# Attention in a fixed order of slots on every engine, four transposed-probability buffers, the query scale in the exponential, and the first three gates on GpSimd

## The chip, the cores and the metric

One core of one Trainium2 chip. Time is device microseconds (us) of the one core, the median of the runs shown; lower is better. The engines of the core are TensorE (PE in the rows; its weight loads PEld), VectorE (DVE), ScalarE (ACT), GpSimd (POOL) and SyncE (SP, which only issues DMAs here).

## What is computed

Three layers in one launch: attention with a mask from hashed buckets, a mixture of eight experts with two experts for each token, and a feed-forward layer with a rational activation. The change lies in the first layer and in the choice of experts.

```python
# attention: q, k, v are [2, 8, 768, 64]; proj is [64, 6]
q_bucket = sum(((q @ proj) > 0) * 2**arange(6)); k_bucket likewise
scores = where(q_bucket[:, :, :, None] == k_bucket[:, :, None, :], 0.125 * q @ k.T, -1e9)
attn = exp(scores - max(scores)); attn = attn / (sum(attn) + 1e-9)
x = (attn @ v).transpose(0, 2, 1, 3).reshape(1536, 512)
# choice of experts, 8 of them
noisy = x @ w_gate + log1p(exp(x @ w_noise)) * noise
top2, weights = the two largest of noisy, and their softmax
x = sum over a token's two experts e: weight * relu(x @ w1[e]) @ w2[e]     # 512 -> 1024 -> 512
# last layer
h = x @ w_in; out = (P(h) / Q(|h|)) @ w_out                                # 512 -> 2048 -> 512
```

## The kernel before

**Precision.** Products are taken in float32r (one pass over PE) with each operand as a high part, rounded, and a low part, the rest; a product is two or three such passes. So nearly every tile is made twice: ACT copies the high part, DVE or GpSimd subtracts it from the original.

**Units and slots.** Attention is cut into 32 units, a head's 384 queries of one batch (a "group" of tokens, four of them), and each unit into three query tiles of 128. One tile is the work of one slot, 96 in all. A tile goes through five stages, each a slot or more after the one before: `score` (4 products of 384 columns, the bucket bits as extra rows of the operands, so that a key of another bucket gets a far lower score), the row maximum and from it scale and bias (`sb`) on DVE, `expo` (the exponential on ACT), then for two of the unit's six key tiles `ptrans` (3 transposes each into one PSUM tile, a copy of the high part on ACT, the low part on DVE, both into a tile `PT`), and `av` (4 products with the values). The PSUM tiles: two for scores (`ps_s`), three small ones (`ps_1`) that transposes, bucket bits and `fold` share, one for the output (`ps_o`).

**Beside the slots.** For each head the keys are split (`k_split`: ACT and GpSimd) and their bits made (`k_bits`, 4 products, one DVE instruction and two DMAs); for each unit the queries are split (`q_split`: GpSimd multiplies by 0.125, ACT copies the high part with the same scale, GpSimd subtracts), and for two units the bits (`q_bits2`, 4 products, one ACT instruction and two DMAs). After a unit's last `av` its output is copied (`oT`), the sums are inverted (`rec`, two DVE instructions), `fold` (3 products) adds high and low parts and makes the gates' columns, and DVE scales them into the rows of the experts (`xg` or `io`). After a group's last head its `Gate` chooses the experts: some 25 small instructions of DVE, 4 of ACT, 7 products, and 6 indirect DMAs of GpSimd that scatter the rows.

**What sets the order.** `run` calls the stages slot by slot; but in attention the order on each engine is set by the compiler's scheduler, which lists instructions by priority and its own times and so may shift one between the instructions of another stage. The order is fixed in the program; at run time each engine goes through its list and waits at the first instruction whose inputs are not there. From the second expert layer's start on the order of PE, ACT and DVE is the program's (`manual_schedule`).

## Time and profile before

| | us |
|---|---|
| median of three runs | 927.43 (927.17 to 929.77) |
| span of the profiled execution, first to last instruction | 918.6 |
| median less span: start and end, outside the span | 8.8 |
| from the first exponential's start to the last one's, 95 slots | 12.5 to 268.6: 256.1 |
| from there to the first product with the first expert's last rows | 268.6 to 284 |
| experts and last layer | 284 to 918.6: 634.6 |

The profiled execution has no time of its own beside its span, so what lies around the span is taken as the median less the span. In the profile, "busy" is the time in which at least one instruction of the engine runs; instructions of one engine can overlap by a little, so that the distance of two starts is shorter than a duration. The mean duration of a group of instructions includes whatever holds one back after it has started.

### The profile page before, as it was taken

Reading aid. Unit: us, or ns where it says so; the run is one execution under the profiler, and the core shown is the slowest. Engines: PE = TensorE matmul, PEld = TensorE weight load, DVE = VectorE, ACT = ScalarE, POOL = GpSimd, SP = SyncE. Lnnn points to the kernel's source line nnn. Section 1 sums busy time; section 2 is a strip of 40 time slices with the busy share of each in tenths; the row PEclk is TensorE's granted clock in tenths of the full one; section 3 lists DMA queues with packets and bytes.
Section 4 is the critical chain, followed back from the end, with each engine's and each line's share of the span. In section 5 each row is a group of like instructions: output and inputs, shape, how many; then the busy total and the mean of one; then the engine's idle time right before and its main releaser. Section 6 shows DMA issues by size and latency. Waiting matters only on the chain. (4 is left out here: it accounts for less than half of the span.)

```text
span 918.6 us, 14182 instructions
## 1 busy us (share of the span) xinstructions
PE 876.3 (95%) x4725; PEld 777.0 (85%) x4725; DVE 772.3 (84%) x1484; ACT 656.2 (71%) x1302; POOL 353.1 (38%) x328
## 2 busy tenths in 40 slices
PE   6999999998999999999999999997989999999997
PEld 4888999898987888888888888876777899989995
DVE  8999999999985777777777776635999999999996
ACT  6888888898973555555545555525988988988885
POOL 6667444644504243433344332032363242222221
PEclk9999999999999999999999999998999999999999
DMA  8888852431313877879687776534221010000000
GB/s 247 229 236 230 265 132 56 151 92 56 131 42 130 252 246 249 252 244 293 224 261 242 231 249 223 177 106 136 71 81 35 36 46 1 36 1 1 35 1 34
DMA packets 89948, 132.22 MB, mean 144 GB/s; under 512 B 9296, under 2 KB 56400, under 8 KB 89872
## 3 DMA queue, kind: packets, MB, share of 16 engines
q1 hardware_dynamic: 86032, 118.70, 41.8%
q0 software_dynamic: 3840, 12.59, 4.3%
q8 instruction: 38, 0.62, 0.3%
q14 instruction: 38, 0.31, 0.1%
HBM read 88.20 MB, written 33.55 MB: 133 GB/s over the span
## 5 line engine op out<-in xcount | busy, mean ns | idle before, releaser
L757 PE MATMUL ps<-xsT,big 128*128 128x448 f32 x768 | 168.2, 368 | 0.0
L776 PE MATMUL s<-big,hT 128*128 128x512 f32 x633 | 154.5, 391 | 0.7 <-DVE hT L762 0.7
L757 PEld LDWEIGHTS ps<-xsT,big 128*128 128x128 f32 x768 | 142.2, 188 | 12.0
L1006 PE MATMUL ps<-x2T,big 128*128 128x384 f32 x768 | 147.5, 340 | 2.8 <-DVEq L891 1.5
L1058 PE MATMUL s<-big,gT 128*128 128x512 f32 x528 | 141.0, 398 | 8.6 <-ACT gT L1041 4.4
L1006 PEld LDWEIGHTS ps<-x2T,big 128*128 128x128 f32 x768 | 137.0, 190 | 8.3 <-ACTq L891 1.9
L1042 POOL TENSOR_TENSOR gT<-uu,gT 128x384 fp32r<-128x384 f32 x64 | 71.7, 1120 | 187.3 <-ACT gT L1041 169.0
L776 PEld LDWEIGHTS s<-big,hT 128*128 128x128 f32 x633 | 118.8, 188 | 23.3 <-DVE hT L762 1.1
L643 DVE TENSOR_TENSOR big<-wraw,big 128x1024 fp32r<-128x1024 f32 x76 | 98.9, 1306 | 36.3 <-ACT big L639 36.3
L1058 PEld LDWEIGHTS s<-big,gT 128*128 128x128 f32 x528 | 96.3, 188 | 33.9 <-ACT gT L1041 9.2
L761 ACT ACTIVATE hT<-ps 128x384 fp32r<-128x384 f32 x114 | 40.7, 357 | 102.3 <-DVE hT L762 82.2
L687 POOL TENSOR_SCALAR convok<-convok 128x512 f32<-128x512 f32 x32 | 49.5, 1546 | 154.8 <-ACT convok L681 150.3
L288 PE MATMUL o<-PT,vhl 128*128 128x384 f32 x384 | 105.3, 368 | 3.2 <-DVE PT L278 2.8
L278 DVE TENSOR_TENSOR PT<-ps,PT 128x384 fp32r<-128x384 f32 x192 | 103.9, 549 | 5.3 <-ACT PT L277 4.2
L267 ACT ACTIVATE probs<-s,sb 128x768 f32<-128x768 f32 x96 | 95.5, 995 | 16.3 <-DVE sb L259 15.3
L277 ACT ACTIVATE PT<-ps 128x384 fp32r<-128x384 f32 x192 | 93.0, 492 | 16.6 <-PE o L288 8.5
L275 PE MATMUL ps<-ident,probs 128*128 128x128 f32 x576 | 95.5, 275 | 5.7 <-DVE PT L278 3.4
L251 PE MATMUL s<-big,qT 128*128 128x384 f32 x384 | 95.2, 362 | 2.9 <-ACT probs L267 1.6
L258 DVE TENSOR_REDUCE mx<-s 128x1 f32<-128x768 f32 x96 | 91.0, 948 | 7.0 <-PE s L251 6.5
L275 PEld LDWEIGHTS ps<-ident,probs 128*128 128x128 f32 x576 | 72.0, 140 | 17.9 <-DVE PT L278 5.2
L639 ACT ACTIVATE big<-wraw 128x1024 fp32r<-128x1024 f32 x80 | 83.9, 1056 | 2.3 <-DMA wraw<-in_moe_w_dram 2.3
L1023 DVE SCALAR_TENSOR_TENSOR uu<-uu,na,hh 128x384 f32<-128x384 f32 x64 | 73.5, 1149 | 1.9
(188 smaller groups left out, 1495.6 us busy)
## 6 DMA issues: line engine op xcount, KB each, us to landing
wraw<-in_moe_w_dram SPq DMA_DIRECT2D x64, 512.0 KB, 5.0
wraw<-in_moe_w_in_dram SPq DMA_DIRECT2D x16, 512.0 KB, 4.9
wraw<-in_moe_w_out_dram SPq DMA_DIRECT2D x16, 512.0 KB, 3.8
xs<-zero SPq DMA_DIRECT2D x14, 512.0 KB, 4.5
io<-xs SPq DMA_DIRECT2D x14, 448.0 KB, 4.6
qraw<-in_q_dram SPq DMA_DIRECT2D x32, 192.0 KB, 2.7
y<-io SPq DMA_DIRECT2D x24, 256.0 KB, 3.4
kraw<-in_k_dram SPq DMA_DIRECT2D x15, 384.0 KB, 3.7
```

The source lines that it names most:

```text
L251: nc.tensor.matmul(ps[:, c, 0:384], T[:, r, q], R[:, r, c * 384:(c + 1) * 384], start=(r == 1), stop=(r == 0))
L258: nc.vector.tensor_reduce(m[:, 1:2], ps[:, :, 0:384], axis=AX.XY, op=ALU.max, negate=True)
L267: nc.scalar.activation(pt.rearrange("p (c k) -> p c k", c=2), ps[:, :, 0:384], AF.Exp, bias=sb[:, 1:2], scale=sb[:, 0:1], accum_out=st["su ...
L275: nc.tensor.transpose(ps[:, i * P:(i + 1) * P], self.S[u]["P"][i][:, kt * P:(kt + 1) * P], E.ident)
L277: nc.scalar.activation(t[:, 0, :], ps[:, 0:384], AF.Copy)
L278: nc.vector.tensor_tensor(t[:, 1, :], ps[:, 0:384], t[:, 0, :].bitcast(F32), op=ALU.subtract)
L288: nc.tensor.matmul(self.O[u][:, 0:384], self.K[b, h]["vhl"][:, kt, :], t[:, r, :], start=(kt == 0 and r == 0), stop=(kt == 5 and r == 1))
L643: (lo or nc.vector).tensor_tensor(t[:, 1, :], raw, t[:, 0, :].bitcast(F32), op=ALU.subtract)
L757: nc.tensor.matmul(ps[:, 0:CAP], w[:, a, c, fs], x[:, c, b, :], start=(n == 0), stop=(n == 11))
L776: nc.tensor.matmul(self.acc[e][j], h[a][:, j * P:(j + 1) * P] if j < 3 else tail, w[:, b, :], start=(f == 0 and a + b == 0), stop=(f == 7 ...
L1006: nc.tensor.matmul(ps, w[:, a, c, fs], x[:, b, c, :], start=(n == 0), stop=(n == 11))
L1058: nc.tensor.matmul(ps, g[:, a, j * P:(j + 1) * P], w[:, b, f % 2, :], start=(f == 0 and a + b == 0), stop=(f == 15 and a == 1))
```

## The change

Five things, all up to the end of attention:

1. **Order.** Attention runs inside `manual_schedule` for PE, ACT, DVE and GpSimd: each slot's instructions stand on each engine in the order in which the loop calls them. Functions that mixed engines are cut so that each part can have its place: `ptrans` into `ptrans`, `high` (ACT) and `low` (DVE), `score` into `score` and `most` (DVE), `q_bits2` and `k_bits` into products and `_out`, `av`'s end into `out` and `recip`, `fold` into `fold` and `rows`, the gates' steps into finer ones. The slots of keys, queries and gates get new rules (`ks`, `vs`, `kb`).
2. **The maximum.** It goes to an unused column of the score's own PSUM tile, and scale and bias come from two instructions in place of one. The constant tiles `mx` go away.
3. **The query scale.** The 0.125 moves into that scale, so `q_split` loses GpSimd's multiplication; `BIG` grows to match.
4. **Buffers.** `PT` has four in place of three; the tile `spacer` moves to a pool that outlives attention.
5. **Gates.** For the first three groups the small elementwise steps run on GpSimd (`self.eng`), some as two instructions where DVE has a fused one; their scatters are one per slot. The split of the last group's rows for the first expert goes head by head.

```diff
+LAG = 1
+PTB = 4
-BIG = float(2 ** 28)
+BIG = float(2 ** 31)
...
     def q_split(self, u, eng=None):
...
-            q = self.ap.tile([P, 384], F32, name="qs", bufs=2)
-            nc.gpsimd.tensor_scalar(q, raw, 0.125, None, op0=ALU.mult)
-            nc.scalar.activation(T[:, 0, :], raw, AF.Copy, scale=0.125)
-            nc.gpsimd.tensor_tensor(T[:, 1, :], q, T[:, 0, :].bitcast(F32), op=ALU.subtract)
+        nc.scalar.activation(T[:, 0, :], raw, AF.Copy)
+        (eng or nc.gpsimd).tensor_tensor(T[:, 1, :], raw, T[:, 0, :].bitcast(F32), op=ALU.subtract)
...
-        m = E.mx[self.nm % len(E.mx)]
-        self.nm += 1
+        self.S[u][i] = ps
+
+    def most(self, u, i):
+        nc, E = self.nc, self.E
+        ps = self.S[u][i]
+        m = ps[:, 0, 384:385]
         sb = self.ap.tile([P, 2], F32, name="sb", bufs=6)
-        nc.vector.tensor_reduce(m[:, 1:2], ps[:, :, 0:384], axis=AX.XY, op=ALU.max, negate=True)
-        nc.vector.scalar_tensor_tensor(sb, m[:, 1:2].to_broadcast([P, 2]), BIG, m,
-                                       op0=ALU.is_le, op1=ALU.mult)
+        nc.vector.tensor_reduce(m, ps[:, :, 0:384], axis=AX.XY, op=ALU.max, negate=True)
+        nc.vector.tensor_scalar(sb[:, 0:1], m, BIG, 0.125, op0=ALU.is_le, op1=ALU.mult)
+        nc.vector.tensor_tensor(sb[:, 1:2], m, sb[:, 0:1], op=ALU.mult)
...
-        t = self.ap.tile([P, 2, 384], F32R, name="PT", bufs=3)
+        self.PT[u, kt] = ps
+
+    def high(self, u, kt):
+        nc, ps = self.nc, self.PT[u, kt]
+        t = self.ap.tile([P, 2, 384], F32R, name="PT", bufs=PTB)
         nc.scalar.activation(t[:, 0, :], ps[:, 0:384], AF.Copy)
+        self.PT[u, kt] = (ps, t)
+
+    def low(self, u, kt):
+        nc, (ps, t) = self.nc, self.PT[u, kt]
         nc.vector.tensor_tensor(t[:, 1, :], ps[:, 0:384], t[:, 0, :].bitcast(F32), op=ALU.subtract)
...
-        for s in range(max(max(pe), max(free), 3 * N + 8) + 1):
-            pend.extend(pe.get(s, []))
-            for f, a in free.get(s, []):
-                f(*a)
-            stage(self.ptrans, s - 4, 2)
-            stage(self.score, s, 1)
-            stage(self.ptrans, s - 4, 2, 1)
-            stage(self.expo, s - 1, 1)
-            stage(self.av, s - 5, 2)
-            misc()
-            stage(self.av, s - 5, 2, 1)
-            misc()
-            while len(pend) > 7:
-                misc()
...
+        with self.tc.manual_schedule(engines=MANUAL | {mybir.EngineType.Pool}):
+            for s in range(max(max(d) for d in (bits, dve, act, outs, free)) + 1):
+                run(free, s)
+                run(outs, s)
+                stage(self.ptrans, s - 4, 2)
+                stage(self.high, s - 4, 2)
+                stage(self.ptrans, s - 4, 2, 1)
+                stage(self.high, s - 4, 2, 1)
+                stage(self.expo, s - 1, 1)
+                run(act, s)
+                stage(self.score, s, 1)
+                run(dve, s)
+                stage(self.low, s - 4, 2)
+                stage(self.low, s - 4, 2, 1)
+                stage(self.most, s, 1)
+                run(bits, s)
+                stage(self.av, s - 4 - LAG, 2)
+                stage(self.av, s - 4 - LAG, 2, 1)
...
+        self.eng = tc.nc.gpsimd if n < 3 else tc.nc.vector
...
         if self.n < 3:
-            return [self.choose, self.noisy, self.top, self.rank, self.rank2, self.scatter]
+            return [(free, 4, self.choose), (act, 4, self.soft), (free, 5, self.noisy), (dve, 6, self.top),
+                    (bits, 7, self.rank), (dve, 7, self.count), (dve, 8, self.rank2), (free, 9, self.weigh),
+                    (act, 10, self.weigh2), (dve, 11, self.weigh3)] + [(free, 10 + i, self.scatter, i) for i in range(6)]
```

The lists `free`, `outs`, `act`, `dve` and `bits` hold what a slot does beside the stages; a gate's pieces stand as (list, slots after its unit's end, function). Three places show what that does to the order. The first is DVE in the middle of a batch of heads. Before, the maximum (L258), `sb` (L259) and the low parts (L278) of different tiles stand between one another:

```order
L278 TENSOR_TENSOR PT<-ps_982,PT 128x384 [waits Activation_49]
L258 TENSOR_REDUCE mx_126<-s 128x1 [waits PE_49]
L278 TENSOR_TENSOR PT<-ps_998,PT 128x384 [waits Activation_49]
L259 SCALAR_TENSOR_TENSOR sb<-mx_126 128x2 [waits DVE_49]
L314 TENSOR_TENSOR lgh<-ps_1009,rec 128x3x16 [waits PE_49]
L319 TENSOR_TENSOR io<-ps_1009,rec 128x2x64
L319 TENSOR_TENSOR io<-ps_1009,rec 128x64
L278 TENSOR_TENSOR PT<-ps_1022,PT 128x384 [waits Activation_49]
L258 TENSOR_REDUCE mx_127<-s 128x1 [waits PE_49]
L278 TENSOR_TENSOR PT<-ps_1037,PT 128x384 [waits Activation_49]
L259 SCALAR_TENSOR_TENSOR sb<-mx_127 128x2 [waits DVE_49]
```

Of the change, at about the same place (L295 is the low part, L266 the maximum, L268 and L269 scale and bias, L201 the keys' bits):

```order
L295 TENSOR_TENSOR PT<-ps_1062,PT 128x384 [waits Activation_49]
L266 TENSOR_REDUCE s<-s 128x1 [waits PE_49]
L268 TENSOR_SCALAR sb<-s 128x1 [waits DVE_49]
L269 TENSOR_TENSOR sb<-s,sb 128x1 [waits DVE_49]
L201 TENSOR_SCALAR big_903<-ps_1084,kthr,kmul 128x384 [waits PE_49]
L295 TENSOR_TENSOR PT<-ps_1096,PT 128x384 [waits Activation_49]
L295 TENSOR_TENSOR PT<-ps_1102,PT 128x384 [waits Activation_49]
L266 TENSOR_REDUCE s<-s 128x1 [waits PE_49]
L268 TENSOR_SCALAR sb<-s 128x1 [waits DVE_49]
L269 TENSOR_TENSOR sb<-s,sb 128x1 [waits DVE_49]
L342 TENSOR_TENSOR lgh<-ps_1128,rec 128x3x16 [waits PE_49]
```

The maximum and the two instructions that make `sb` now follow each other directly, and each of the two waits for the DVE instruction ahead of it. The second place is PE in a slot with the bits of a head's keys (L193) and of two units' queries (L234), of the change (L284 transposes, L255 scores, L305 `av`):

```order
L284 MATMUL ps_928<-ident,probs 128x128 [waits DVE_49,PE_49]
L284 MATMUL ps_928<-ident,probs 128x128 x2
L284 MATMUL ps_934<-ident,probs 128x128 [waits DVE_49]
L284 MATMUL ps_934<-ident,probs 128x128 x2
L255 MATMUL s<-big_410,qT 128x384 [waits Activation_49]
L255 MATMUL s<-big_410,qT 128x384 x3
L193 MATMUL ps_956<-big_779,pj 128x384 [waits DMAHW1_49,DVE_49,Pool_49]
L193 MATMUL ps_956<-big_779,pj 128x384 x3
L234 MATMUL ps_961<-qT,pj 128x384 [waits DVE_49]
L234 MATMUL ps_961<-qT,pj 128x384 x2
L234 MATMUL ps_961<-qT,pj 128x384 [waits Pool_49]
L305 MATMUL o<-PT,vhl 128x384 [waits Activation_49]
```

Before, keys' bits stand between the two halves of `av` (L288; L275 are transposes, L251 scores):

```order
L275 MATMUL ps_788<-ident,probs 128x128 [waits DVE_49,PE_49]
L275 MATMUL ps_788<-ident,probs 128x128 x2
L288 MATMUL o<-PT,vhl 128x384 [waits Activation_49]
L288 MATMUL o<-PT,vhl 128x384
L193 MATMUL ps_799<-big_676,pj 128x384 [waits DMAHW6_49,DVE_49]
L193 MATMUL ps_799<-big_676,pj 128x384 x3
L288 MATMUL o<-PT,vhl 128x384 [waits Activation_49]
L288 MATMUL o<-PT,vhl 128x384
```

What moved: transposes, scores and `av` are now blocks of six, four and four, and both kinds of bits stand behind the scores and ahead of `av`; six of the slots have both, and in these four tiles of `ps_1` are asked for. The third place is GpSimd at the first gate, of the change (L481 to L500 are the gate's, L218 the queries' low part, L177 the keys', L158 and L159 the values'); before, nothing of the gates but the scatters is on GpSimd:

```order
L158 CAST vhl<-vraw 128x6x64 [waits DMAHW5_49]
L159 TENSOR_TENSOR vhl<-vraw,vhl 128x6x64 [waits Pool_49]
L481 TENSOR_TENSOR lg<-lg,lgh 128x48 [waits DVE_49]
L496 TENSOR_SCALAR gb<-lg 128x24 [waits Pool_49]
L497 TENSOR_TENSOR gb<-gb,noise_sb 128x24 [waits Pool_49]
L500 TENSOR_TENSOR gb<-gb,lg 128x24 [waits Pool_49]
L500 TENSOR_TENSOR ga<-ga,noise_sb 128x24 [waits Activation_49]
L500 TENSOR_TENSOR ga<-ga,gb 128x24 [waits Pool_49]
L218 TENSOR_TENSOR qT<-qraw,qT 128x384 [waits DMAHW4_49,DMAHW7_49,PE_49,Activation_49]
```

So six of a gate's small steps stand there between the splits, each waiting for the one before, and queries' low parts stand behind them.

## Rows read from the trace of the kernel before

**Rows 1.** The page: busy us of each engine, with its share of the span.

```profile
PE 876.3 (95%) x4725; PEld 777.0 (85%) x4725; DVE 772.3 (84%) x1484; ACT 656.2 (71%) x1302; POOL 353.1 (38%) x328
```

**Rows 2.** Busy time of each engine by stretch (start:end, length, busy).

```profile
12.50:268.60 256.10, 243.24 (x1617) 224.23 (x1618) 242.36 (x620) 220.81 (x479) 136.17 (x123) 1.00 0.53 156
268.60:284.00 15.40, 12.93 (x92) 10.70 (x91) 11.21 (x51) 6.08 (x16) 6.88 (x10) 1.00 0.01 2
284.00:918.60 634.60, 613.52 (x3000) 536.83 (x2999) 508.54 (x765) 423.29 (x798) 205.83 (x166) 0.99 0.44 141
```

**Rows 3.** DVE's groups, 12.5 to 268.6: count, busy, mean ns, idle before.

```profile
L278 DVE TENSOR_TENSOR PT<-ps,PT 128x384 fp32r<-128x384 f32 x184 | 99.6, 549 | 4.2 <-ACT PT L277 3.1
L258 DVE TENSOR_REDUCE mx<-s 128x1 f32<-128x768 f32 x95 | 90.0, 948 | 6.6 <-PE s L251 6.0
L259 DVE SCALAR_TENSOR_TENSOR sb<-mx 128x2 f32<-128x2 f32 x95 | 31.1, 327 | 0.0
L196 DVE TENSOR_SCALAR big<-ps,kthr,kmul 128x384 fp32r<-128x384 f32 x14 | 9.3, 667 | 0.0
L295 DVE TENSOR_SCALAR rec<-sums 128x3 f32<-128x3 f32 x30 | 8.9, 303 | 0.2 <-ACT probs L267 0.2
```

**Rows 4.** Timeline, 51 to 53.6, of DVE, GpSimd and the exponential: start, length.

```profile
51.43 1.84 POOL L177 TENSOR_TENSOR big<-kraw,big 64x768 fp32r<-64x768 f32 x1
51.59 1.69 DVE L259 SCALAR_TENSOR_TENSOR sb<-mx 128x2 f32<-128x2 f32 x1
...
53.32 0.99 ACT L267 ACTIVATE probs<-s,sb 128x768 f32<-128x768 f32 x1 [1.21 <-DVE sb L259]
```

**Rows 5.** Timeline of DVE, 143.8 to 145.4.

```profile
143.85 0.15 DVE L259 SCALAR_TENSOR_TENSOR sb<-mx 128x2 f32<-128x2 f32 x1
143.92 0.55 DVE L278 TENSOR_TENSOR PT<-ps,PT 128x384 fp32r<-128x384 f32 x1
144.39 0.95 DVE L258 TENSOR_REDUCE mx<-s 128x1 f32<-128x768 f32 x1
145.25 0.17 DVE L296 RECIPROCAL rec<-rec 128x3 f32<-128x3 f32 x1
```

**Rows 6.** Timeline of DVE, 282.3 to 282.8: the last gate's chain.

```profile
282.39 0.17 DVE L488 SCALAR_TENSOR_TENSOR sl<-pos,sl 128x6 f32<-128x6 f32 x1
282.59 0.17 DVE L489 TENSOR_TENSOR sl<-sl,ovf 128x6 f32<-128x6 f32 x1
```

**Rows 7.** DVE's small groups of three gates: the longest and the shortest that move.

```profile
L445 DVE TENSOR_TENSOR gb<-gb,lg 128x24 f32<-128x24 f32 x3 | 1.2, 389 | 0.0
...
L489 DVE TENSOR_TENSOR sl<-sl,ovf 128x6 f32<-128x6 f32 x3 | 0.5, 150 | 0.0
```

**Rows 8.** Timeline of PE, 99.3 to 106.8.

```profile
101.31 0.85 PE L193 MATMUL ps<-big,pj 128*128 128x384 f32 x4
102.00 0.51 PE L288 MATMUL o<-PT,vhl 128*128 128x384 f32 x2
...
103.45 0.49 PE L275 MATMUL ps<-ident,probs 128*128 128x128 f32 x3
103.70 0.95 PE L288 MATMUL o<-PT,vhl 128*128 128x384 f32 x4
104.49 0.49 PE L275 MATMUL ps<-ident,probs 128*128 128x128 f32 x3
...
106.19 0.79 PE L312 MATMUL ps<-fold,oT 128*128 128x80 f32 x6
106.78 0.59 PE L288 MATMUL o<-PT,vhl 128*128 128x384 f32 x2
```

**Rows 9.** GpSimd's and ACT's groups, 12.5 to 268.6.

```profile
L217 POOL TENSOR_SCALAR qs<-qraw 128x384 f32<-128x384 f32 x28 | 32.8, 1172 | 2.0
...
L158 POOL CAST vhl<-vraw 128x384 fp32r<-128x384 f32 x14 | 7.7, 550 | 14.4 <-PE o L288 11.3 <-DMA vraw<-in_v_dram 2.8
...
L277 ACT ACTIVATE PT<-ps 128x384 fp32r<-128x384 f32 x185 | 89.6, 492 | 15.0 <-PE o L288 8.0 <-PE ps L275 5.0
```

More of the change, by code (lines that the diff above doesn't have):

```diff
@@ L80, in constants @@
     nc.vector.memset(E.nearly, -(1.0 - 2.0 ** -23))
-    E.mx = [ap.tile([P, 2], F32, name=f"mx{i}", bufs=1) for i in range(6)]
-    for m in E.mx:
-        nc.vector.memset(m, 1.0)
     E.jp = jp
@@ L118, in gate_constants @@
     nc.vector.memset(E.carry[0], 0.0)
-    E.spacer = ap.tile([1, 1], F32, name="spacer", bufs=1)
+    E.spacer = cp.tile([1, 1], F32, name="spacer")
     E.zero = E.att_pool.tile([P, 128], F32, name="zero", bufs=1)
@@ L289, in av, with out, recip, rows @@
                              start=(kt == 0 and r == 0), stop=(kt == 5 and r == 1))
-        if kt == 5:
-            o = self.ap.tile([P, 384], F32, name="oT", bufs=2)
-            nc.scalar.activation(o, self.O[u][:, 0:384], AF.Copy)
-            self.O[u] = o
-            rec = self.ap.tile([P, 3], F32, name="rec", bufs=2)
-            nc.vector.tensor_scalar(rec, self.S[u]["sum"], 1e-9, None, op0=ALU.add)
-            nc.vector.reciprocal(rec, rec)
-            self.S[u] = rec
-    def fold(self, u):
+    def out(self, u):
+        nc = self.nc
+        o = self.ap.tile([P, 384], F32, name="oT", bufs=2)
+        nc.scalar.activation(o, self.O[u][:, 0:384], AF.Copy)
+        self.O[u] = o
+    def recip(self, u):
+        nc = self.nc
+        rec = self.ap.tile([P, 3], F32, name="rec", bufs=2)
+        nc.vector.tensor_scalar(rec, self.S[u]["sum"], 1e-9, None, op0=ALU.add)
+        nc.vector.reciprocal(rec, rec)
+        self.S[u] = rec
+    def fold(self, u):
+        nc, E = self.nc, self.E
+        b, g, h = self.units[u]
+        ps = E.ps_1.tile([P, 512], F32, name="ps1")
+        o = self.O.pop(u)
+        for i in range(3):
+            nc.tensor.matmul(ps[:, i * 80:(i + 1) * 80], o[:, i * P:(i + 1) * P], E.fold[:, h, :], start=True, stop=True)
+        self.O[u] = ps
+    def rows(self, u):
         nc, E = self.nc, self.E
@@ L308, in fold @@
             self.lg[b, g] = self.ap.tile([P, 3, H, 16], F32, name="lgh", bufs=3)
-        ps = E.ps_1.tile([P, 512], F32, name="ps1")
-        o, rec = self.O.pop(u), self.S.pop(u)
-        for i in range(3):
-            nc.tensor.matmul(ps[:, i * 80:(i + 1) * 80], o[:, i * P:(i + 1) * P], E.fold[:, h, :], start=True, stop=True)
+        ps, rec = self.O.pop(u), self.S.pop(u)
         pv = ps[:, 0:240].rearrange("p (i d) -> p i d", i=3)
@@ L326, in run @@
         N = len(self.units)
-        pe, free = {}, {}
+        bits, dve, act, outs, free = ({} for _ in range(5))
         def at(d, slot, f, *a):
@@ L371, in run @@
         for u in range(N):
-            at(pe, 3 * u + 8, self.fold, u)
+            e = 3 * u + 6 + LAG
+            at(outs, e + 1, self.out, u)
+            at(dve, e + 1, self.recip, u)
+            at(bits, e + 2, self.fold, u)
+            at(dve, e + 3, self.rows, u)
             b, g, h = self.units[u]
             if h == 6:
-                at(pe, 3 * u + 10, gates[b, g].most)
+                at(dve, e + 3, gates[b, g].most)
+            if b and g:
+                at(free if h < 7 else act, e + 4, E.first.split, h)
@@ L428, in most @@
                                      axis=AX.X, op=ALU.add)
-        if self.n == 3:
-            self.first = self.E.first
-            self.first.split(slice(0, 448))
     def choose(self):
@@ L435, in choose, with soft @@
         lg = self.lg
-        if self.n == 3:
-            self.first.split(slice(448, 512))
-        nc.vector.tensor_add(lg, lg, self.att.lg[self.key][:, :, 7, :])
+        self.eng.tensor_tensor(lg, lg, self.att.lg[self.key][:, :, 7, :], op=ALU.add)
+    def soft(self):
+        nc, E, pool, tt, lg = self.nc, self.E, self.pool, self.tt, self.lg
         self.a = a = pool.tile([P, 3, 8], F32, name="ga", bufs=2)
```

159 lines of the change are left out of this document (93 added, 66 removed).

## The prediction

> **What bounds the kernel now.** I read first the page's line of busy times, then the busy times by stretch, then DVE's groups and its timeline, then PE's. Over the whole span PE looks like the bound with 95%, and DVE follows with 84% [rows 1]. By stretch it is different: from 284 us on PE is busy for 613.5 of 634.6 us, and the change touches nothing there. In the 256.1 us between the first and the last exponential PE and DVE are busy for 243.2 and 242.4 us, ACT for 220.8, GpSimd for 136.2 [rows 2]. Two engines at 95% that wait for each other: this is the stretch to work in. DVE has 13.7 us without work there, and its groups say for what it waits then: scores (6.0), high parts of `PT` (3.1) and a few more [rows 3].
>
> Busy is not the same as needed. On PE, starts tell more than durations: three transposes take 0.25 us (103.45 to 103.70), four products of 384 columns 0.79 (103.70 to 104.49), bits 0.69, a unit's `fold` 0.59 [rows 8]. A slot needs 2 x 0.25 + 2 x 0.79 = 2.08 us, at most; with 0.78 for a scores' block that I read beside it, 2.05. So 95 slots take 195 us, 30 `fold` 18, 28 products of bits 19.5, in all 232: PE could be 24 us faster than it is. On DVE the suspicious group is `sb`, two numbers for each row, at 327 ns on average [rows 3], where an undisturbed one takes 150 [rows 5]. The row at 51.59 shows the reason: it lasts 1.69 us and ends as GpSimd's keys, begun just before, end [rows 4]; the exponential behind it waits for 1.21 us. The instructions that read PSUM show nothing of this: 549 and 948 ns on average [rows 3], as in a stretch without such a collision [rows 5], although GpSimd is busy for half the time. So 95 x (327 - 152) = 16.6 us of DVE's busy time is waiting for GpSimd.
>
> The Trainium skill has the rule (SBUF — State Buffer, Who interferes with whom): a DVE instruction contends with GpSimd if both its inputs lie in SBUF or if it runs in a two-port mode, and the one that comes second waits for the whole instruction of the other. The trace agrees: the old `sb` reads SBUF alone, and 1.69 us is what was left of GpSimd's 1.84.
>
> **The change, part by part,** against the profiled execution: span 918.6 us, and 8.8 us around it by the median of 927.43.
>
> *The maximum in PSUM.* Each of the two new instructions reads the maximum from PSUM and at most one tile from SBUF, as L278 does, which nothing delays. I take all 16.6 us as gone.
>
> *The chain.* Now the price. An instruction that needs nothing of the one ahead starts 0.08 to 0.09 us before that one ends: 143.85 to 143.92 is 0.07 for a `sb`, 144.39 to 145.25 is 0.86 for a maximum [rows 5]. One that needs it starts 0.03 after its end: 282.39 to 282.59 is 0.20 for an instruction of 0.17 [rows 6]. Before, the scheduler mostly put a low part between the maximum and `sb`, so a tile cost 0.86 + 0.07 = 0.93 us of DVE. Now they follow each other: 0.95 + 0.03 for the maximum, 0.15 + 0.03 for the scale, 0.07 for the bias, in all 1.23 to 1.24. For 95 tiles that is 117.8 us. Before, the two groups' durations are 121.1 us with the holds [rows 3]; less 0.083 for each of 190 starts, 105.3, if every one had its overlap. So the net of hold and chain is 12.5 us more at most, and less by 0.1 us or so for each start that had no overlap; I let one in eight have had none, and take 10.0: the holds' 16.6 gone, 26.6 paid. Whether a maximum written to PSUM takes longer than one written to SBUF, no row shows. From below: nothing. From above: 0.05 a tile, as `lgh` of 48 columns at 200 ns against 150 of small ones, 4.8 us. I take nothing, since the width explains those 0.05.
>
> *Gates.* Fourteen groups of three leave DVE, from 389 to 150 ns on average [rows 7], 2.98 us together for a gate, 8.9 for three, less 0.08 for each of 42 starts: 5.5 us gone. The three pairs of largest value and index are now chained one by one, nine times 0.11, 1.0 us more. On GpSimd they become some 16 instructions for each gate; no row has such a small one, so from nothing to the 0.55 of a copy of 384 columns [rows 9], 0 to 26 us in all. GpSimd has 120 us without work here and loses 28 multiplications, 32.8 us [rows 9]. Should it be late all the same, queries' low parts stand behind the gate on its list, and PE's bits wait for these; but they are asked for three slots later. The choice of the largest two, on DVE, comes two slots after the gate's first step.
>
> *Query scale.* GpSimd's 32.8 us are off the path, since GpSimd mostly waits for ACT. ACT's copy stays. `rec` (303 ns, 150 undisturbed) still reads SBUF alone and still collides, at most as often as before: 0 to 4.5 us gone, I take 1.
>
> *Buffers.* ACT waits 8.0 us for `av` to free a `PT` tile [rows 9]. ACT is 35 us short of full, so this alone brings nothing; it helps DVE in as far as L278 waits for ACT (3.1 us, in the idle time below).
>
> *DMAs and the rest.* Every DMA is issued as often as before; SyncE's list is still the scheduler's, bits are asked for three slots or more ahead of their score. PE waited for one once, 1.1 us; I leave that. The 15.4 us after the last exponential are the same chain of the last gate [rows 2]; split and spacer change nothing that it waits for, 0, within 1 us either way.
>
> So DVE needs 242.4 + 10.0 - 5.5 + 1.0 - 1.0 = 246.9 us for the stretch: **4.5 us more than before**, against 232 of PE. Whether the change gains hangs on the 13.7 us of idle time.
>
> *The waits that are left.* Take a slot in the new order, from the end of its second low part on. DVE goes through chain, extras, two low parts: 1.24 + 0.93, 2.17, and 0.59 (keys' bits) or 0.3 (`rec`) or 0.45 (rows) on top. PE takes 0.25 + 0.78 + 0.70 + 0.79 + 0.25 with one block of bits, and until the next high part is there 0.24 for the last product, 0.49 for ACT and some 0.2 for four hand-overs like the 0.04 from 53.28 to 53.32 [rows 4]: 3.7 us, where DVE, two chains, `rec`, bits and two low parts on, comes to it after 4.3. So DVE finds its inputs. It does not where a slot has both blocks of bits: the second one asks for a fourth small PSUM tile and waits for the low part that frees one, at 1.24 + 0.30 + 0.55 = 2.1 us, and then 0.70 + 0.79 + 0.25 + 0.24 + 0.49 + 0.2 to the high part, 4.75 against 4.3. That is 0.45 in each of six slots, 2.7 us. One more for filling the first slots, one for ACT, whose key splits stand ahead of high parts with hardly a margin. I take 4.8 us, 9 less than now. The time is then 918.6 + 4.5 - 8.9 + 8.8 = 923.0; with PSUM's unknown leaning the other way I say **923.5**.
>
> **The rivals.** "Same" is within 0.3%, 2.8 us, about what this kernel's measurement can tell from no change.
>
> *The chain without the gain (slower).* DVE's longer chain is sure, the emptier queue is not: if each late input stops DVE as often as now, in its fixed list of slots, the idle time stays at 13.7, and 927.43 + 4.5 = 931.9, up to 936 with PSUM's 4.8. It decides from an idle time of 9.2 us on; below that the change gains. For it speaks that nothing can stand between a late high part and the rest of a slot any more; against it, that PE has 24 us to spare and that the long random holds of `sb`, which empty the pipeline today, are gone. 0.24.
>
> *Half of it (same).* Idle time of 7 to 12 us, 924.7 to 929.7. 0.28.
>
> *Chaining costs nothing (much faster).* If each instruction costs its start-to-start time whatever stands behind it, the three cost 0.86 + 0.07 + 0.07 = 1.00 a tile, 95 against 117.8 us, and DVE needs 224; PE's 232 and some 12 us of waits then give 918.6 - 12 + 8.8, 915. Against it stand the 0.20 of [rows 6], with two starts of many alike. 0.12.
>
> [...]
>
> **How the numbers follow.** The forecast (idle time under 7 us, 918 to 924.7, most of it near 923.5) has 0.36, the rivals 0.24, 0.28 and 0.12. Faster by over 0.3%: the forecast and the last rival, 0.47; same 0.29, slower 0.24. The range from 913 to 934 leaves out the upper part of the slower case and half of the much faster one, less than 2 in 10. The likeliest case's own is 919 to 925.
>
> **What would show it.** In the profile after: the group of the scale at about 155 ns with no long ones, and of the bias alike, right or wrong on the collision; the start of the scale 0.98 after that of the maximum, and the next low part 1.23 to 1.24 after it, on the chain; DVE busy for some 247 us between the first and last exponential and idle for under 7, on the forecast; waits of DVE for PE's high parts or scores of 0.4 us in the slots with both bits, on the six. The stretch should take 252 us, and the 634.6 us behind it should not move. The forecast is wrong if DVE's idle time is over 9 us, or if a maximum into PSUM takes longer than 0.95.

## The result and the profile after

The changed kernel takes 939.52 us (median of four runs, 937.98 to 941.59) where the kernel before took 928.60 beside it: a ratio of 1.0126 [1.0101 to 1.0152], slower (the two medians divided give 1.0118, inside the interval). A second set of runs gave 1.0136 [1.0111 to 1.0160]. The prediction, 923.5 with a range up to 934, was wrong.

Busy time by stretch of the changed kernel, columns as in [rows 2]:

```profile
12.32:287.57 275.25, 250.38 (x1622) 233.87 (x1623) 248.72 (x676) 220.29 (x481) 118.44 (x180) 0.98 0.49 144
287.57:303.00 15.43, 12.65 (x84) 10.57 (x83) 11.20 (x49) 6.44 (x16) 6.69 (x14) 0.93 0.11 38
303.00:939.70 636.70, 615.64 (x3007) 539.11 (x3006) 511.48 (x771) 423.46 (x799) 206.21 (x171) 0.99 0.44 140
```

The loss is all in the first row: 275.3 us against 256.1 in [rows 2]; the 15.4 behind it stayed, and 636.7 against 634.6 is what executions differ by (638.7 in the other one of before, below). In that row DVE is busy for 248.7 us, near the forecast's 247, and idle for 26.5, where the forecast had under 7. DVE's groups in this stretch, as in [rows 3]:

```profile
L295 DVE TENSOR_TENSOR PT<-ps,PT 128x384 fp32r<-128x384 f32 x185 | 93.9, 547 | 10.0 <-ACT PT L290 9.5 <-issue 0.2
L266 DVE TENSOR_REDUCE s<-s 128x1 f32<-128x768 f32 x95 | 90.9, 957 | 0.5 <-PE s L255 0.3
L268 DVE TENSOR_SCALAR sb<-s 128x1 f32<-128x1 f32 x95 | 15.0, 158 | 3.3
L269 DVE TENSOR_TENSOR sb<-s,sb 128x1 f32<-128x1 f32 x95 | 15.0, 157 | 3.3
L317 DVE TENSOR_SCALAR rec<-sums 128x3 f32<-128x3 f32 x30 | 10.2, 340 | 0.0
...
L581 DVE TENSOR_SCALAR gr<-gd 128x3 f32<-128x3 f32 x3 | 2.4, 792 | 0.0
```

Scale and bias take 158 and 157 ns with no long one among them: GpSimd's holds of `sb` are gone, as said. The 3.3 us ahead of each are the 0.035 that a chained instruction starts after the end of the one before. What the forecast called need holds such gaps, the idle time of the profile too; so from here on both are counted alike, from the starts of all DVE instructions in the stretch: the distance from a start to the next is **need**, except that idle time over 0.06 us in it is a **stop**. So need and stops together are the stretch. "Chain" is the need of the 95 maxima, scales and biases, "gates" that of all the gates' steps that are on DVE. All in us:

| | stretch | stops | need | chain | `rec` | gates |
|---|---|---|---|---|---|---|
| before, as profiled ahead | 256.1 | 13.1 | 243.0 | 108.2 | 11.3 | 11.7 |
| before again | 259.6 | 17.8 | 241.8 | 107.9 | 10.7 | 11.4 |
| forecast | 251.7 | 4.8 | 246.9 | 117.8 | | |
| changed | 275.3 | 17.9 | 257.4 | 120.9 | 14.6 | 10.8 |
| changed again | 274.6 | 17.5 | 257.1 | 120.7 | 14.6 | 10.8 |

So two terms failed: the need rose by about 14 us and not by 4.5, and the stops did not fall to 4.8. Of the 23.6 us by which the stretch missed its forecast, 13.1 are stops and 10.5 need.

Where the stops are, the waits of DVE in the stretch say (total, times, longest):

```profile
DVE PT L295 <- ACT PT L290: 9.5, 22, 1.8
DVE na L1028 <- DMA ab<-in_moe_a_dram: 4.3, 1, 4.3
DVE big L201 <- PE ps L193: 1.6, 1, 1.6
DVE qT L218 <- ACT qT L217: 1.3, 1, 1.3
```

By slot, the 17.9 are: 5.5 in the first seven slots; 4.3 at `na`; 2.0 in seven slots with a key split on ACT; 1.8 in the six slots with both blocks of bits; 2.8 in two slots of the first gates; the rest in small ones. The longest, DVE's timeline:

```profile
84.47 0.16 DVE L317 TENSOR_SCALAR rec<-sums 128x3 f32<-128x3 f32 x1
88.90 0.17 DVE L1028 TENSOR_SCALAR na<-ab 128x4 f32<-128x4 f32 x1 [4.27 <-DMA ab<-in_moe_a_dram]
88.98 0.17 DVE L318 RECIPROCAL rec<-rec 128x3 f32<-128x3 f32 x1
```

`na` is a constant of the last layer, written in the program after attention (`Last.constants`). It lies outside the fixed order, so the scheduler may put it anywhere, and put it between two instructions of one `rec`; its DMA was issued at 82.48 behind 512 KB loads of weights. The engine waits at it with everything behind. The Trainium skill states it (PSUM — Partial Sum Buffer, Engine vs sequencer instructions): the queues of ScalarE, VectorE and GpSimd are strictly first in, first out. The trace agrees: the RECIPROCAL behind `na` had its input from 84.63 on and started at 88.98. PE waited for 3.4 us meanwhile, and the step from one exponential to the next was 6.4 us.

The start, busy time in two stretches of the changed kernel, then of another execution of the kernel before:

```profile
15.00:20.00 5.00, 3.73 (x13) 3.12 (x12) 4.49 (x11) 3.72 (x7) 0.00 (x0) 0.50 0.85 255
25.00:30.00 5.00, 3.37 (x16) 3.31 (x17) 1.82 (x5) 0.60 (x2) 0.00 (x0) 0.79 0.90 286
```

```profile
15.00:20.00 5.00, 4.75 (x22) 4.33 (x21) 4.23 (x9) 3.34 (x7) 4.75 (x6) 0.66 0.72 195
25.00:30.00 5.00, 4.87 (x30) 4.06 (x29) 4.89 (x12) 5.00 (x11) 2.84 (x2) 1.00 0.91 271
```

After, GpSimd does nothing in either. In the first, DVE splits the second head's keys itself, some 1.5 us; in the second it waits for the bits of the third head's keys, whose products PE could not start earlier (timeline of the changed kernel):

```profile
26.63 0.94 PE L193 MATMUL ps<-big,pj 128*128 128x384 f32 x4 [2.68 <-DMA big<-big]
```

The first eight slots take 25.7 us against 18.0. The stop in the first of the two gate slots begins at ACT, which waits for GpSimd's first step of the gate:

```profile
178.50 0.22 ACT L486 ACTIVATE ga<-lg 128x24 f32<-128x24 f32 x1 [1.21 <-POOL lg L481]
```

### The profile page after: what moved, and what is told of

The parts are those of the page before. It is cut to its first block, busy times and chain, and to the rows that moved or that the text cites. A ratio compares the mean times of both kernels' runs of the same rounds, so it can differ in the third digit from the quotient of the medians.

```text
span 939.7 us, 14199 instructions
## 1 busy us (share of the span) xinstructions
PE 884.3 (94%) x4725; PEld 788.0 (84%) x4725; DVE 780.8 (83%) x1532; ACT 655.1 (70%) x1304; POOL 333.6 (35%) x373
## 5 line engine op out<-in xcount | busy, mean ns | idle before, releaser
L290 ACT ACTIVATE PT<-ps 128x384 fp32r<-128x384 f32 x192 | 85.4, 496 | 40.9 <-PE ps L284 40.4
L295 DVE TENSOR_TENSOR PT<-ps,PT 128x384 fp32r<-128x384 f32 x192 | 97.5, 548 | 12.0 <-ACT PT L290 11.5
L276 ACT ACTIVATE probs<-s,sb 128x768 f32<-128x768 f32 x96 | 95.9, 999 | 10.7 <-DVE sb L269 9.8
L255 PE MATMUL s<-big,qT 128*128 128x384 f32 x384 | 94.3, 368 | 4.0 <-ACT probs L276 3.8
L284 PE MATMUL ps<-ident,probs 128*128 128x128 f32 x576 | 84.4, 279 | 12.3 <-DVE PT L295 7.9
L266 DVE TENSOR_REDUCE s<-s 128x1 f32<-128x768 f32 x96 | 91.9, 957 | 1.1 <-PE s L255 0.9
L284 PEld LDWEIGHTS ps<-ident,probs 128*128 128x128 f32 x576 | 69.1, 143 | 22.4 <-DVE PT L295 11.3
L305 PE MATMUL o<-PT,vhl 128*128 128x384 f32 x384 | 86.7, 348 | 0.6 <-ACT oT L311 0.6
```

The lines of the kernel that those rows point to most:

```text
L255: nc.tensor.matmul(ps[:, c, 0:384], T[:, r, q], R[:, r, c * 384:(c + 1) * 384], start=(r == 1), stop=(r == 0))
L266: nc.vector.tensor_reduce(m, ps[:, :, 0:384], axis=AX.XY, op=ALU.max, negate=True)
L276: nc.scalar.activation(pt.rearrange("p (c k) -> p c k", c=2), ps[:, :, 0:384], AF.Exp, bias=sb[:, 1:2], scale=sb[:, 0:1], accum_out=st["su ...
L284: nc.tensor.transpose(ps[:, i * P:(i + 1) * P], self.S[u]["P"][i][:, kt * P:(kt + 1) * P], E.ident)
L295: nc.vector.tensor_tensor(t[:, 1, :], ps[:, 0:384], t[:, 0, :].bitcast(F32), op=ALU.subtract)
L305: nc.tensor.matmul(self.O[u][:, 0:384], self.K[b, h]["vhl"][:, kt, :], t[:, r, :], start=(kt == 0 and r == 0), stop=(kt == 5 and r == 1))
```

## The experiments

Ratios are to the kernel before, run beside each on the same chip; "less" and "more" in us are against the changed kernel at 1.0131, the mean of its two, times 927, and uncertain by some 3 us.

For six runs that is not all of the uncertainty. The kernel before took 926.0 to 928.6 us on most chips, but 923.2 on the chip of the first four runs of "The parts, one by one", and 922.5 on that of the run with the gates' steps alone and of the last run; the changed kernel was not timed beside these. There the medians, taken as they are against the changed kernel's 939.5, give 4 to 6 us less than the ratios do, and the profiled stretches (275.0 for the changed kernel, the mean of its two) side with the medians. The rest of the span, outside the stretch, was no shorter on those two chips (661.3 to 666.4 us, 660.7 to 667.2 on the others). Whether the changed kernel would be quicker there too, which the ratios suppose, stays open; so these runs have all three numbers.

### One execution more of each kernel

> The changed kernel once more, with a profile, beside the kernels of this call. All theories: 1.010 to 1.015 of the kernel before; DVE's stops of over 0.06 us between the first and last exponential should again make 15 to 20 us of the stretch, if they belong to the order and not to one execution, with the two longest at the third head's key bits (some 3 us) and at na (1 to 4.3).

1.0136; stops of 17.5 us, as in the first execution, so they are not one execution's chance.

> The kernel before once more, with a profile. If the profiled execution of before (918.6 us, where its timed runs lie near 927) was a quick one, the stretch between the first and the last exponential is now 258 to 264 us in place of 256.1, by more stops of DVE; if the 636 us behind it vary instead, the stretch is again 256.

928.58 us with a span of 926.8; stretch 259.6. Its stops are 17.8 us, 4.7 more than in the execution that the prediction read, so 13.7 us of idle time was the lower of two samples; against this one the changed kernel's stretch is 15 us longer and not 19. The two longest new stops are 2.40 and 1.99 us. Around the first, timeline of this run:

```profile
185.75 0.97 POOL L505 DMA_INDIRECT xs<-xg,slot  x1 [0.31 <-issue]
...
186.50 0.96 DVE L258 TENSOR_REDUCE mx<-s 128x1 f32<-128x768 f32 x1 [2.40 <-PE ps L312]
186.74 1.00 POOL L219 TENSOR_TENSOR qT<-qs,qT 128x384 fp32r<-128x384 f32 x1
...
188.01 0.87 ACT L277 ACTIVATE PT<-ps 128x384 fp32r<-128x384 f32 x2 [2.81 <-remote]
```

A queries' low part stands behind six scatters on GpSimd, and ACT, PE and DVE go on only after it (PE after 2.60 us, DVE after 1.07). That they waited for it is likely and not shown: "remote" is an end that the profile can't place. The stop of 2.40 had ended before the low part began, and what ended it stays open.

### The parts, one by one

```diff
-            last.constants()
             with tc.manual_schedule(engines=MANUAL):
                 ex.run_last(last)
+                last.constants()
```

> The constants of the last layer are made at the end of the last expert layer, so that the small DVE instruction na no longer stands in attention's list (nothing is left out). Few long stops: its wait of 4.27 us for a DMA, during which PE and ACT stood still too, is a loss of its own, so 939.5 - 4.3 = 935.2 us, and the step from the exponential at 85.3 to the next one falls from 6.5 to about 2.5 us. Rival, longer chain in every slot: DVE catches up after any stop and other waits take its place, within 1 us of 939.5.

1.0104, 2.5 us less; by medians 6.2 less (933.27), in the stretch 8.6 (266.4), where stops fell from 17.9 to 9.5. Direction and place as expected; of the size only that the expected 4.3 lies between.

```diff
-                kb = 5
+                kb = 7
```

> The bits of the third head's keys are asked for in slot 7 in place of slot 5 (nothing is left out). Few long stops: PE no longer waits 2.68 us for the copy of these keys, nor DVE 1.61 and 1.49 us behind it, so 3 us less, 936.5, and up to 2 more if the granted clock stays at 1.00 between 25 and 35 us (it was 0.79 and 0.87). Rival, the start is held by its DMAs anyway: the wait only moves two slots on, where scores of that head or bits of queries wait for it, and the time stays within 1 us of 939.5.

1.0197, 6 more; by medians 0.9 more (940.43), in the stretch 1.9 less (273.1). By none of them the 3 us less that were expected: the rival, or worse. The start took nearly as long (24.7 us for eight slots against 25.7), a stop of 1.35 stood in the eighth, and `rec`, at other times relative to GpSimd now, was held more (18.9 us of need against 14.6).

```diff
-        self.eng = tc.nc.gpsimd if n < 3 else tc.nc.vector
+        self.eng = tc.nc.vector
```

> The first three gates' small steps go back to DVE, still in pieces at the same slots (nothing is left out). As the prediction priced it, DVE gets 42 instructions of 0.15 us at about 0.13 each from start to start back, 5.5 us: 945.0. Rival, the gates on GpSimd cost more than they give, since queries' low parts stand behind them and the two instructions for gr are held by GpSimd (0.79 us on average): DVE gets the 5.5 but loses 2 us of holds and some 4 us of waits in the slots from 50 to 63, so 937 to 940.

1.0208, 7 more; by medians 1.8 more (941.29), in the stretch 2.2 (277.2). The gates' need on DVE is 17.1 us against 10.8, so GpSimd does take 6.3 us off DVE, about as expected; in this profile the stops were 4.9 shorter, and most of it did not reach the stretch. And 17.1 for the steps that took 11.7 in the scheduler's order: nine instructions more, since what DVE has fused stands as two, are some 1.8 of it; for the rest, standing next to each other they wait for each other.

```diff
-        nc.vector.tensor_tensor(sb[:, 1:2], m, sb[:, 0:1], op=ALU.mult)
+        nc.vector.tensor_scalar(sb[:, 1:2], m, 0.125, 60.0, op0=ALU.mult, op1=ALU.min)
```

> The bias is worked out from the maximum alone (times 0.125, at most 60), so that it no longer waits for the scale; only for rows without any key of their bucket does the number differ, and there every value of it gives the same weights. The start of the bias comes 0.08 in place of 0.19 us after that of the scale, 0.11 less in each of 95 slots. Longer chain in every slot (DVE is the bound all the time): 10.4 us less, 929. Few long stops: only slots in which DVE sets the pace gain, and stops are as long as before; since nearly all slots without a stop are of that kind here, 6 to 9 less, 930.5 to 933.5, with DVE's idle time of stops as long as now (18 us by gaps over 0.06).

1.0069, 5.8 less; by medians 11.8 less (927.71), in the stretch 12.8 (262.2). The chain fell from 120.9 to 109.0, with stops nearly as long as before (16.9). So in the profile the 11.9 us of need came off whole, as the theory of the longer chain has it; by the ratio half of them did, as that of few long stops has it. These times don't decide between the two.

```diff
                 stage(self.low, s - 4, 2)
-                stage(self.low, s - 4, 2, 1)
-                stage(self.most, s, 1)
+                stage(self.most, s, 1)
+                stage(self.low, s - 4, 2, 1)
+                stage(self.scale, s, 1)
```

(`most` is cut in two for this: the maximum, and `scale` with scale and bias.)

> The second low part stands between the maximum and the scale (nothing is left out): the scale no longer waits for the instruction just ahead of it. From start to start a tile's chain should cost 0.86 for the maximum, 0.19 for the scale and 0.09 for the bias in place of 0.99, 0.19 and 0.09. Longer chain in every slot: 0.13 x 95 = 12 us less than the changed kernel. Few long stops: the low part now stands ahead of the scale and, where its high part is late, holds up the exponential as well, so only slots without a stop gain, 6 to 10 us less. Rival, order alone: nothing, since PE and ACT set the pace of a slot (within 2 us of the changed kernel).

1.0187, 5 more: all three theories wrong. The chain fell to 108.7 as worked out, but its stops rose to 29.9. DVE's groups of this run show why:

```profile
L298 DVE TENSOR_TENSOR PT<-ps,PT 128x384 fp32r<-128x384 f32 x185 | 101.2, 547 | 17.6 <-ACT PT L293 16.1 <-issue 0.4
L266 DVE TENSOR_REDUCE s<-s 128x1 f32<-128x768 f32 x95 | 91.1, 959 | 4.7 <-PE s L255 3.4 <-issue 0.3
```

A low part that waits for ACT now holds up scale and bias, and so the exponential on ACT itself. It is not enough that DVE has less to do.

### Order and maximum apart

The kernel before, with the maximum alone changed, and then the changed kernel with the maximum and the scale put back (for its two instructions, GpSimd's multiplication and `BIG` too):

```diff
-        m = E.mx[self.nm % len(E.mx)]
+        m = ps[:, 0, 384:385]
...
-        nc.vector.scalar_tensor_tensor(sb, m[:, 1:2].to_broadcast([P, 2]), BIG, m,
-                                       op0=ALU.is_le, op1=ALU.mult)
+        nc.vector.tensor_scalar(sb[:, 0:1], m, BIG, 1.0, op0=ALU.is_le, op1=ALU.mult)
+        nc.vector.tensor_tensor(sb[:, 1:2], m, sb[:, 0:1], op=ALU.mult)
```

> The kernel before with the maximum in PSUM and scale and bias by two instructions, and nothing else of the change; the scheduler still sets the order, and puts low parts and rows between the three. If the maximum in PSUM is a gain and only the fixed order's direct chain a loss: the holds of 16.6 us go, 95 short instructions of 0.07 to 0.19 from start to start come, so DVE needs 5 to 10 us less, and the time is 0.990 to 0.997 of the kernel before. Rival, the maximum in PSUM with two instructions is itself the loss: 1.005 to 1.012.

1.0126: just over the rival's range, without its mechanism. Need fell to 239.4 (the chain from 108.2 to 99.5, while the gates rose from 11.7 to 15.4), but the scheduler put out another order, whose stops are 33.3 us, as DVE's waits show:

```profile
DVE PT L277 <- ACT PT L276: 11.4, 24, 2.2
DVE s L257 <- PE s L251: 5.7, 13, 0.7
DVE na L957 <- DMA ab<-in_moe_a_dram: 2.8, 1, 2.8
DVE s L257 <- PE ps L311: 2.6, 1, 2.6
```

So a change of two instructions alone made a list that waits, and the kernel before owes part of its time to one that waits little.

```diff
-        m = ps[:, 0, 384:385]
+        m = E.mx[self.nm % len(E.mx)]
...
-        nc.vector.tensor_scalar(sb[:, 0:1], m, BIG, 0.125, op0=ALU.is_le, op1=ALU.mult)
-        nc.vector.tensor_tensor(sb[:, 1:2], m, sb[:, 0:1], op=ALU.mult)
+        nc.vector.scalar_tensor_tensor(sb, m[:, 1:2].to_broadcast([P, 2]), BIG, m,
+                                       op0=ALU.is_le, op1=ALU.mult)
```

> The changed kernel with the maximum and the query scale as before (one instruction for sb, from SBUF; GpSimd multiplies the queries); the fixed order, four buffers and the gates on GpSimd stay. If the fixed order with its stops is most of the loss: a tile's chain is 0.98 + 0.07 and a hold of some 0.18, 1.23 in place of 1.27, so about 4 us less than the changed kernel, 1.007 of the kernel before; with more holds, since GpSimd works 33 us more, as slow as the changed kernel. Rival, the maximum's two instructions are the loss: back to the kernel before, 0.997 to 1.003.

1.0129, as slow as the changed kernel, which the expectation held open for more holds. They came; its groups of `sb` and of the maximum:

```profile
L277 DVE SCALAR_TENSOR_TENSOR sb<-mx 128x2 f32<-128x2 f32 x95 | 43.4, 457 | 3.3
L276 DVE TENSOR_REDUCE mx<-s 128x1 f32<-128x768 f32 x95 | 89.9, 946 | 0.8 <-PE s L264 0.5 <-PE ps L293 0.3
```

457 ns against 327 in [rows 3]: `sb` meets GpSimd more often here (37 of 95 took over 0.25 us, 22 before). Whether by the fixed order or by the gates' steps that GpSimd now has, this run doesn't separate. Chain 129.9, stops 16.6. In this order the maximum in PSUM is worth 9 us of the chain, and 7 of them are taken back at `rec` (9.2 of need here, 14.6 in the changed kernel) and the gates (9.1 and 10.8).

### The holds at `rec`

```diff
-        nc.vector.tensor_scalar(rec, self.S[u]["sum"], 1e-9, None, op0=ALU.add)
-        nc.vector.reciprocal(rec, rec)
+        nc.vector.reciprocal(rec, self.S[u]["sum"])
...
-        nc.vector.tensor_scalar(r, d, 1.0, 1e-9, op0=ALU.add, op1=ALU.add)
+        self.eng.tensor_scalar(r, d, 1.0, 1e-9, op0=ALU.add, op1=ALU.add)
```

> The sums are inverted without the addition of 1e-9 (left out; a sum is 1 or more, where float32 can't hold it anyway), and the gates' gr is made by GpSimd, so that neither instruction is left on DVE to be held by GpSimd. 5.5 us of holds at rec, 1.8 at gr, and 30 short instructions go from DVE's list. Longer need of DVE is the loss: 7 to 11 us less than the changed kernel, 1.002 to 1.006 of the kernel before. Rival, as in the run with the low part between: DVE's need falls and its stops grow by as much, within 3 us of the changed kernel.

1.0140, no gain, but not for the rival's reason. Its own second edit made new waits:

```profile
DVE gw L581 <- POOL gr L580: 11.7, 3, 4.3
```

On GpSimd's list `gr` stood behind a queries' low part in two gates (which itself waited for ACT, once for 4.03 us), and behind a split of weights and a scatter in the third; DVE waited for it each time. Inconclusive, so the first half was run alone:

> As the run without holds, but gr stays on DVE: only the addition of 1e-9 at the sums is left out. If the 11.6 us of waits for gr behind GpSimd's scatters hid the gain: the changed kernel less 5 to 8 us (holds of 5.5 at rec and a chained short instruction in 32 slots; less 16 slots which PE holds at 2.85 us anyway), 1.004 to 1.008 of the kernel before. Rival, shorter lists of DVE only become stops, as with the low part between: 1.011 to 1.015.

1.0051, 7.4 less, as expected. Need 245.9, stops 17.4.

### Several mended

> na at the end, the bias from the maximum alone, no rec addition, gr by GpSimd (left out: the 1e-9 at the sums). If each is a loss of its own: 2 to 4, 6 to 9 and 7 to 11 us less than the changed kernel, 16 to 22 together, 0.990 to 0.996 of the kernel before. Rival, with DVE's need down to some 240 us PE and the chain of waits between the engines set the pace: half of it, 1.000 to 1.005.

1.0075; it has the same `gr`, with 11.3 us of waits. Without that:

> na at the end, the bias from the maximum alone, no addition at the sums, gr on DVE. If each is a loss of its own: the run of the three less the 11 us that gr on GpSimd cost it, 0.994 to 0.998 of the kernel before. Rival, with the three gone PE and GpSimd set the pace: 1.002 to 1.006.

0.9988 [0.9973 to 1.0004], 13 less: short of 0.994 to 0.998. Need fell by 22 us to 235.2, and stops rose to 24.9.

```diff
+            eng = nc.gpsimd if b + h else nc.vector
...
-                nc.vector.tensor_copy(R[:, 1, c], raw[:, c])
+                eng.tensor_copy(R[:, 1, c], raw[:, c])
...
-                nc.vector.tensor_tensor(R[lo, 0, c], raw[lo, c], R[lo, 1, c].bitcast(F32), op=ALU.subtract)
+                eng.tensor_tensor(R[lo, 0, c], raw[lo, c], R[lo, 1, c].bitcast(F32), op=ALU.subtract)
...
-            at(act, max(3 * u - 9, u - 2), self.q_split, u, nc.vector if u < 4 else None)
+            at(act, max(3 * u - 9, u - 2), self.q_split, u)
```

> At the start the second head's keys and two units' queries are split by GpSimd in place of DVE (nothing is left out). If the fixed order's list on DVE makes the start slow (first eight slots in 25.7 us, 18.3 before): DVE's 1.35 us stop and four instructions of 2.6 us go, so 3 to 5 us less than the changed kernel. Rival, DMAs and the lower granted clock of TensorE bound the start: within 1 us.

Alone 1.0108, 2 less, within the uncertainty; its first eight slots take 22.9 us.

> The three, and the start's splits on GpSimd. If the slow start is a loss of its own: 2 to 4 us less than the three alone, 0.990 to 0.995. Rival, the start is made up for by slot 24, as the step from slot 8 to 16 in the changed kernel suggests (4 us of the first 7 come back): within 1 us of the three.

0.9939, 4.5 less than the three: a loss of its own.

```diff
+            o = 13 if self.n == 1 else 10
-            return [(free, 4, self.choose), (act, 4, self.soft), (free, 5, self.noisy), (dve, 6, self.top),
+            return [(free, 4, self.choose), (act, 5, self.soft), (free, 6, self.noisy), (dve, 7, self.top),
...
-                    (act, 10, self.weigh2), (dve, 11, self.weigh3)] + [(free, 10 + i, self.scatter, i) for i in range(6)]
+                    (act, 11, self.weigh2), (dve, 12, self.weigh3)] + [(free, o + i, self.scatter, i) for i in range(6)]
```

> As before it, and the first gates' steps from the logarithm on one slot later (ACT waited 1.2 us for GpSimd's first step), the second gate's scatters three slots later, so that they no longer fall on the first one's and hold queries' low parts. If the stops between slots 50 and 64 are GpSimd's list: 3 to 5 us less than with the start alone, 0.986 to 0.991. Rival, they are the six slots with both bits: within 1 us.

0.9892 [0.9870 to 0.9913], 916.29 us: faster than both kernels. Stretch 250.9:

```profile
11.88:262.73 250.85, 241.94 (x1620) 230.75 (x1621) 228.59 (x642) 218.51 (x481) 123.35 (x185) 0.99 0.55 157
```

> The changed kernel with the gates' steps from the logarithm on one slot later and the second gate's scatters three slots later, nothing else. If the stops between slots 50 and 64 are GpSimd's list, they are a loss of their own here too: 3 to 5 us less than the changed kernel, 1.007 to 1.010 of the kernel before. Rival, with DVE's longer list its own work fills these slots, and the gain needs the other mends: 1.012 to 1.015.

1.0135, no gain, the rival; by medians 4.8 less (934.73), in the stretch 5.0 (270.0), with stops of 13.5: the 3 to 5 that were expected. What the gates' stops cost by themselves stays open.

```diff
+            if j > 2 and kb % 6 == 2:
+                kb -= 1
```

> The kernel with the three, the start and the gates mended, and keys' bits one slot earlier wherever they fell in one slot with queries' bits. If a slot with both blocks of bits is long because PE and a fourth small PSUM tile are short there (3.2 to 3.5 us against 2.85 with one block, stops of DVE of 0.35 to 0.72, six times): 2 to 4 us less, 0.985 to 0.987 of the kernel before. Rival, the bits only move PE's work into the slots with rows, and these become longer: within 1 us, 0.988 to 0.990.

0.9884, within 1 us of 0.9892: the rival's number (912.47 us, on another chip; the stretch is 249.2, 1.7 less). From one exponential to the next, five of the six slots fell from 3.3 to 3.7 us to 2.8, and one stayed at 3.2; the slot ahead of three of them rose from 2.1 to 2.8, as the rival has it. But part of the gain went elsewhere: 3.2 us less up to slot 57, and 2.0 more in the two slots behind it, near a gate.

A stop of the kind that is left in the better kernel, in a slot with queries' bits; ACT and DVE in the run with the gates mended:

```profile
42.41 0.99 ACT L277 ACTIVATE probs<-s,sb 128x768 f32<-128x768 f32 x1
...
43.37 0.84 ACT L176 ACTIVATE big<-kraw 128x768 fp32r<-128x768 f32 x1
...
44.11 0.49 ACT L312 ACTIVATE oT<-o 128x384 f32<-128x384 f32 x1
...
44.48 0.88 ACT L291 ACTIVATE PT<-ps 128x384 fp32r<-128x384 f32 x2
...
45.01 1.02 DVE L296 TENSOR_TENSOR PT<-ps,PT 128x384 fp32r<-128x384 f32 x2 [0.62 <-ACT PT L291]
45.22 1.02 ACT L277 ACTIVATE probs<-s,sb 128x768 f32<-128x768 f32 x1
```

ACT goes without a gap from one exponential to the next, 2.81 us, since a key split and an `oT` fall into one slot. DVE waits for 0.62. That the split has a better slot was not tried.

## Why the prediction was wrong

**The maximum in PSUM, and holds: right, but for one place.** No scale or bias was held. The maximum takes 957 ns against 948 [rows 3], so PSUM costs 0.9 us in all; "longer than 0.95", a sign of being wrong, was met by so little, and isn't what failed. But `rec` was taken to fall by 1 us, and its need rose by 3.3: 1.1 of it is more hold, the rest that its two instructions now stand next to each other and the second waits for the first. Such a hold, timeline of the changed kernel:

```profile
121.25 1.83 POOL L177 TENSOR_TENSOR big<-kraw,big 64x768 fp32r<-64x768 f32 x1 [1.91 <-issue]
...
121.41 1.70 DVE L317 TENSOR_SCALAR rec<-sums 128x3 f32<-128x3 f32 x1
```

**The chain: right mechanism, size a little off.** Forecast +10.0, measured +12.7 of need (120.9 against 108.2). 0.99 + 0.19 + 0.09 is 1.27 a tile where 1.23 to 1.24 was said. That chaining costs nothing is refuted: in the run with the bias alone the bias starts 0.08 us after the scale, in the changed kernel 0.19. The Trainium skill (VectorE: DVE Perf Modes, The DRAIN you can't avoid) says of eight copies, 13.88 us in all, that a semaphore behind each costs nothing extra. In these rows, for instructions of 0.16 us, waiting for the one ahead costs 0.11, and they decide here.

**Gates: the gain on GpSimd right, the sum wrong.** The 5.5 us that GpSimd takes were measured as 6.3, with those nine instructions more. But the need of the gates fell by 0.9 (11.7 to 10.8) and not by 4.5, since what stays on DVE is now chained and `gr` is held (792 ns): the chain was priced at the row maximum and at the gates' three pairs, and left out at `rec` and at the gates' other steps. So of the 10.5 us of need that were missed 3.1 are the chain's, 4.3 `rec`'s and 3.6 the gates', less 0.5 in the rest.

**The idle time: the step that failed.** "I take 4.8 us, 9 less than now" was worked out from a steady slot. There it was near: six slots with both bits at 0.45 were forecast as 2.7 and cost 1.8. One us for filling the first slots was 5.5, one for ACT 2.0, and `na` (4.3) and the gates' slots (2.8) were not in the sum. "Every DMA is issued as often as before" was true and beside the point: what counts is where the instruction that waits for one now stands. The "long random holds of `sb`, which empty the pipeline" went, and stops of other kinds took the place of the old ones. DVE's waits for scores, 6.0 us in [rows 3], did go, but with the order and not with the holds: the fixed order with the maximum put back has holds and 0.5 of these waits, the scheduler's order with the maximum in PSUM has no holds and 5.7.

**The rival that came true** is the chain without the gain (0.24), with the idle time higher than its 13.7 and the need 10 us more than its 4.5, so that its 931.9 to 936 was missed as well. The 636.7 us behind did not move, as said. Of the 8.8 us "around the span" 1.9 are outside it (941.59 less 939.7 after); the rest was the difference between that execution and the median.

Shown by runs: `rec` with its holds (7.4 us), the start (4.5) and the gates' slots (4.4) with the others mended. The chained bias (5.8 by ratio, 11.8 by medians) and `na` (2.5 and 6.2, plain in the trace) are losses too, of a size left open; added together to a kernel run beside it they gave 5.8 us in one pair of runs (931.16 to 925.40) and 5.9 in another (938.99 to 933.12). What the gates' slots cost alone is open.

## What to carry to other kernels

Price a fixed order by going through its list from the first slot on, not by one steady slot: the start, each rare block, and every instruction from outside that can land in the list. Where an instruction is chained to the one ahead, look for an input that comes earlier (the bias from the maximum) before looking for something to put between: what stands between can wait too. And profile the kernel before twice; the idle time to be gained was 13 us in one execution and 18 in the next. Where variants are compared, run the kernel that they start from on the same chip as well.

## What the runs showed of the hardware

- GpSimd's hold depends on the operation. `rec`'s first instruction (TENSOR_SCALAR, three columns, one input, from SBUF) took up to 1.74 us, six of 30 over 0.25; the RECIPROCAL behind it, also from SBUF to SBUF, never more than 0.18 in any of these runs, nor in the seven in which it stands first and reads the sums itself. The Trainium skill (SBUF — State Buffer, Who interferes with whom) lists copies, casts and tensor_scalar as able to take the shared port with one input, and leaves reciprocal unnamed; the trace agrees with the first.
- TensorE's clock fell at the start of the changed kernel: it waited for 1.9 and 1.3 us behind exponentials, up to 13.5 and 17.0, and was granted 0.50 between 15 and 20 us (1.2 of 2.4 GHz), then 0.79 between 25 and 30, with a wait of 2.7 us that ended at 26.6. In the execution of before shown ahead it was 1.00 in the whole stretch [rows 2]; but in the other one it was 0.66 between 15 and 20, so that the fixed order is not alone in this, and in the changed kernel's second execution 0.85 and 0.67 in the two windows.
